# Raw weights in smaller paced transfers, 64-row products in chunk 0's joins, and sums of squares ahead of turned keys, in a fused DeltaNet and SiLU MLP kernel

## The chip, the cores and the metric

The kernel runs on one core of a Trainium2 chip. The metric is the device time of one execution in microseconds (us). Before the change the median of 3 runs is 650.97 us (650.86 to 651.51).

## What is computed

A DeltaNet recurrence over 768 tokens for 4 batches of 8 heads with 48 dimensions, and then a two-layer MLP with SiLU on all 3072 tokens (384 to 2048 to 384).

```python
k_n = k / (np.linalg.norm(k, axis=-1, keepdims=True) + 1e-06)
for t in range(S):
    kt, vt, bt = (k_n[:, :, t], v[:, :, t], beta[:, :, t, None])
    y[:, :, t] = np.einsum('bhd,bhde->bhe', q[:, :, t], state)
    v_old = np.einsum('bhde,bhd->bhe', state, kt)
    state = state + bt[:, :, :, None] * np.einsum('bhd,bhe->bhde', kt, vt - v_old)
x = y.transpose(0, 2, 1, 3).reshape(B * S, H * D)
h = x @ w_in
out = (h * (1.0 / (1.0 + np.exp(-h)))) @ w_out
```

## The kernel before

The tokens go in 6 chunks of 128, each in two halves of 64 (`hf`); the heads of all batches, 32 of them, go in two groups `g` of 16. Within a half the recurrence is solved in closed form: the products of the keys with each other (`score`, L519) form a triangular matrix per head, its inverse is built, and `inner`, `update`, `keys`, `old` and `new` then are matrix products with it. For chunk 0 the inverse starts from blocks of 16 by 16 on VectorE (`invert_first`, the pairs of operations at L666 and L670), which `joins` puts together to 32 by 32 and then to 64 by 64 on TensorE. Its stages follow one another for a half: `corner` of both groups (L707, evacuated at L714), `turned` of both (L723), `straight` (L736) and `merge_half` (L796), the last in two steps. Every stage's products go to PSUM; ScalarE (`by_act`) and VectorE (`by_dve`) copy the results out, and the next stage reads the copies. `corner`, `turned` and `straight` use 32-row operands: tiles `low`, `y` and `up` in a spare part of `sums_of_w`. One call of `corner` or `straight` has 32 products, of `turned` and `merge_half` 16.

`joins(0)` is run before any chunk's output; `joins(1)` is run in steps between other work. After `joins(0)` come `inner` (L830) and `first_outputs` (L874), and then the first products of the MLP (`hidden`, L1031).

Before the inversion, chunk 0's keys are squared on GpSimd (L375), summed on VectorE (`add_squares`, L379), and turned to norms (`norm_steps`, L393 to L413), of which `spread` goes through a product (`block_steps`, `pg`, L435) to the tile `step` that the inversion scales with. The keys are turned on TensorE (`turn`, L490) and copied out by VectorE (L502) or ScalarE (L504); `first_blocks` (L1274) multiplies them in blocks, and one transpose of VectorE (L1281) brings the blocks in. `busy` (L338) is a product that nobody reads; it fills TensorE's time.

The weights come as raw pairs of 32-bit words. `fetch_w_in` and `fetch_w_out` load piece `i` (768 KB) with one DMA into a buffer that happens to be free: a buffer of the hidden layer, half of a `w_out` buffer, or `sums_of_g`. `narrow` makes float32 of a piece in five steps: two on ScalarE (L226, L227), two on VectorE (L231, L235), one on GpSimd (L239). All loads are issued by SyncE in one line (`in_line`); `pace` makes the next one wait until the DMA before it has landed, and `linked` sets that for one transfer (L170 to L174).

The order of every engine's instructions is that of the program text: `pin` ties each to the one before it on its engine. In the middle of the program a long string of words, written by hand, gives that order (`script`): `s` a step of chunk 0's solution, `f` a step of narrowing, `r` a step of the MLP, `j` a product of `joins(1)`, `T` and `q` the turning of chunk 1's keys and queries, `l`, `p`, `i`, `m`, `t`, `z` steps of chunk 1's and 2's preparation and of the sums of weights. Chunks 1 to 5 follow in loops, with their own order.

Of the kernel before, what the change touches and what calls it, by code (L numbers as in the profile page):

```python
# [19 lines left out]
def kernel(  # L20
# [10 lines left out]
    nc = tc.nc  # L31
# [139 lines left out]
    def linked(fetch, *args):  # L171

        pace.append(line[-1])
        fetch(*args)  # L174

# [100 lines left out]
    def fetch_w_in(i):  # L276
# [8 lines left out]
        in_line(nc.sync.dma_start(out=raw, in_=src))  # L285
# [5 lines left out]
    def fetch_w_out(i):  # L291
# [5 lines left out]
        in_line(nc.sync.dma_start(out=raw, in_=src))  # L297
# [354 lines left out]

    def invert_first(step):
# [7 lines left out]
        for m in range(Q - 1, 0, -1):  # L661
# [39 lines left out]
        def corner(g, hf):  # L701

            pls = [bank(room, "pl") for room in (A, CC)]
            for i, n, k in heads(g, hf):
                for j in (2 * k, 2 * k + 1):
                    cols = slice(T * (j % 2), T * (j % 2 + 1))
                    pin(nc.tensor.matmul(  # L707
                        pls[k][rows[j], Q * i : Q * (i + 1)], lhsT=aps[0, g][0][rows[j], n % HH // H, n % H, cols],
                        rhs=low[rows[j], n, :], start=True, stop=True,
                    ))  # L710
                    yield
            for k in range(2):
                of = slice(W * k, W * (k + 1))
                pin(nc.vector.scalar_tensor_tensor(  # L714
                    out=of_half(y[of], g, hf, k)[:, :, 0:Q], in0=out_of(pls[k], of, Q), scalar=second[of],
                    in1=pick[of, 0:Q].unsqueeze(1).to_broadcast([W, HH // 2, Q]), op0=ALU.mult, op1=ALU.add,
                ))

        def turned(g, hf):

            pls = [bank(room, "pl") for room in (A, CC)]
            for i, n, k in heads(g, hf):
                pin(nc.tensor.matmul(  # L723
                    pls[k][rows[2 * k], T * i : T * (i + 1)], lhsT=up[rows[2 * k], n, :],
                    rhs=y[rows[2 * k], n, :], start=True, stop=True,
# [5 lines left out]
        def straight(g, hf):  # L731

            pls = [bank(room, "pl") for room in (A, CC)]
            for i, n, k in heads(g, hf):
                for j in (2 * k + 1, 2 * k):
                    pin(nc.tensor.matmul(  # L736
                        pls[k][rows[j], T * i : T * (i + 1)], lhsT=y[rows[j], n, :],
                        rhs=up[rows[j], n, :], start=True, stop=True,
                    ))
                    yield  # L740
# [568 lines left out]
    for t in xis:  # L1309
        pin(nc.gpsimd.memset(t, 0.0))  # L1310
    first_sizes = norm_steps(0)
# [4 lines left out]
    pools["m0"] = pools["m1"] = ctx.enter_context(tc.tile_pool(name="hiddens", bufs=1, space=PSUM))  # L1316
    fetch_w_in(0)
    load_k(1)
    fetch_w_in(1)
    load_v(0)  # L1320
    for c in range(1, NCH):
        beta_of(c)
    for b in range(2):
        first_score(b)
    busy(1)
# [261 lines left out]
```

## Time and profile before

| what | value |
|---|---|
| median of 3 runs | 650.97 us (650.86 to 651.51) |
| the profiled execution's own time | 653.34 us |
| its span | 651.4 us |
| granted TensorE clock, mean | 0.976 |
| PE busy (matmul) | 627.3 us, 96% |
| PEld busy (weight loads) | 550.7 us, 85% |
| DVE (VectorE) busy | 394.3 us, 61% |
| ACT (ScalarE) busy | 216.3 us, 33% |
| POOL (GpSimd) busy | 95.7 us, 15% |
| DMA | 53.68 MB, mean 82 GB/s |

Times in the profile are in us from the span's start unless they are marked ns. A row of the timeline has start, duration, engine, line, operation, result and operands, shape and count, and in brackets the idle time before it and what ended it. The releaser "issue" means that the engine waited for nothing that the profile shows. A window's row gives the busy time of each engine in a stretch. One product of 32-bit data appears as two matmuls and two weight loads; a transpose appears as one of each.

### The profile page before, as it was taken

The page shows a single profiled execution, that of the slowest core. Times are in us where ns is not written, and L with a number is a line of the kernel's source. Part 1 is how long each engine was busy: PE and PEld are TensorE (multiplying, and loading weights), DVE is VectorE, ACT ScalarE, POOL GpSimd, SP SyncE. Part 2 cuts the span into 40 slices and gives each one's busy share as a digit, 9 for nine tenths or more (in the row PEclk, how much of TensorE's full clock was granted, in tenths as well). Part 3 has the DMA queues.
Part 4 walks back from the last instruction along what each step waited for, and adds up shares of the span by engine and source line. Part 5 has one row for each costly group of instructions (what it writes and reads, how often), then busy time and mean ns, then how long its engine had stood idle before and what let it go on. Part 6 is the DMA issues. An engine that isn't in the chain of part 4 may idle for free.

```text
span 651.4 us, 21809 instructions
## 1 busy us (share of the span) xinstructions
PE 627.3 (96%) x9644; PEld 550.7 (85%) x9644; DVE 394.3 (61%) x902; ACT 216.3 (33%) x505; POOL 95.7 (15%) x96
## 2 busy tenths in 40 slices
PE   6859999999999999999999999999999999899997
PEld 4648778666789988989989989989989989789997
DVE  5955979988764985554975453986455963103112
ACT  1646666251351122451122451122451122351111
POOL 5231730337011020010020010020011000000000
PEclk9758999999999999999999999999999999999999
DMA  9675444160369433269243259334163023100101
GB/s 171 141 185 149 148 123 105 49 146 3 78 129 155 60 77 46 60 131 159 43 94 34 57 126 151 59 77 50 41 140 71 24 68 43 40 13 1 25 0 25
DMA packets 141310, 53.68 MB, mean 82 GB/s; under 512 B 112912, under 2 KB 134672, under 8 KB 141216
## 3 DMA queue, kind: packets, MB, share of 16 engines
q1 hardware_dynamic: 140880, 52.14, 40.1%
q8 instruction: 76, 1.25, 0.8%
q10 hardware_dynamic: 336, 0.15, 0.1%
q14 instruction: 18, 0.15, 0.1%
HBM read 39.62 MB, written 10.49 MB: 77 GB/s over the span
## 4 chain that ended last, share of the span: by engine, by line
PE 85%; DVE 8%; DMA 2%; issue 2%; ACT 1%; SPq 1%; POOL 0%; DVEq 0%; POOLq 0%
PE phid L1031 35%; PE px L1138 15%; PE py L1138 11%; PE po L1066 7%; PE pa L519 3%; PE pz L830 3%; DVE rank L617 2%; PE pu L850 2%; PE ph L818 2%; DVE x L622 2%; PE pyc L909 2%; PE pt L490 1%; PE pyc L896 1%; PE px L772 1%; PE py L772 1%
## 5 line engine op out<-in xcount | busy, mean ns | idle before, releaser
L1031 PE MATMUL phid<-xT,w_in 128*128 128x256 f32 x1152 | 258.4, 382 | 2.0 <-DMA xT<-part 2.0
L1031 PEld LDWEIGHTS phid<-xT,w_in 128*128 128x128 f32 x1152 | 215.9, 190 | 33.4 <-issue 3.5
L1041 ACT ACTIVATE gT<-phid 128x512 f32<-128x512 f32 x88 | 52.6, 598 | 143.6 <-PE phid L1031 140.8
L617 DVE SCALAR_TENSOR_TENSOR rank<-g,step,x 128x31 f32<-128x31 f32 (+15 forms) x124 | 49.8, 401 | 35.6 <-DMA g<-blocks 32.2
L1120 DVE TENSOR_TENSOR sums_of_g<-gT 128x384 f32<-128x384 f32 (+1 forms) x60 | 30.1, 521 | 58.9 <-ACT gT L1041 48.3
L1138 PE MATMUL px<-sums_of_w,sums_of_g 128*128 128x192 f32 x320 | 56.8, 329 | 0.0
L1138 PE MATMUL py<-w_out,sums_of_g 128*128 128x192 f32 x320 | 56.8, 329 | 0.0
L1138 PEld LDWEIGHTS px<-sums_of_w,sums_of_g 128*128 128x128 f32 x320 | 52.2, 190 | 0.5
L1138 PEld LDWEIGHTS py<-w_out,sums_of_g 128*128 128x128 f32 x320 | 52.2, 190 | 0.4
L622 DVE TENSOR_TENSOR x<-x,rank 128x31 f32<-128x31 f32 (+15 forms) x124 | 42.5, 342 | 4.3
L457 POOL TENSOR_TENSOR vf<-vf,n_slot 128x768 f32<-128x768 f32 x10 | 15.3, 1539 | 174.5 <-DMA vf<-in_v_dram 123.4
L478 DVE STREAM_TRANSPOSE kq<-stage 128x512 f32<-128x512 f32 x28 | 28.6, 1114 | 8.1 <-DMA stage<-in_q_dram 7.6
L534 ACT COPY xT<-pyc 48x128 f32<-48x128 f32 (+2 forms) x126 | 32.6, 259 | 1.6
L1138 PE MATMUL px<-sums_of_w,gT 128*128 128x192 f32 x160 | 28.4, 329 | 0.0
L1138 PE MATMUL py<-w_out,gT 128*128 128x192 f32 x160 | 28.4, 329 | 0.0
L1138 PE MATMUL px<-w_out,gT 128*128 128x192 f32 x160 | 28.0, 327 | 0.0
L830 PEld LDWEIGHTS pz<-vf,xi 64*64 64x64 f32 x768 | 25.2, 142 | 3.2 <-issue 2.9
L540 POOL COPY g<-x 64x256 f32<-64x256 f32 x4 | 5.0, 1240 | 151.9 <-DVE x L625 151.9
L1138 PEld LDWEIGHTS px<-w_out,gT 128*128 128x128 f32 x160 | 26.4, 190 | 0.5
L830 PE MATMUL pz<-vf,xi 64*64 64x48 f32 x768 | 26.9, 226 | 0.0
L1138 PEld LDWEIGHTS py<-w_out,gT 128*128 128x128 f32 x160 | 26.1, 190 | 0.3
L1138 PEld LDWEIGHTS px<-sums_of_w,gT 128*128 128x128 f32 x160 | 26.1, 190 | 0.2
(197 smaller groups left out, 833.8 us busy)
## 6 DMA issues: line engine op xcount, KB each, us to landing
vf<-in_v_dram SPq DMA_DIRECT2D x48, 96.0 KB, 3.3
out_dram<-o SPq DMA_DIRECT2D x42, 96.0 KB, 2.2
w_out<-in_moe_w_in_dram SPq DMA_DIRECT2D x4, 768.0 KB, 6.0
sums_of_w<-in_moe_w_out_dram SPq DMA_DIRECT2D x4, 768.0 KB, 4.9
blocks<-ap SPq DMA_DIRECT2D x40, 64.0 KB, 1.9
g<-blocks SPq DMA_DIRECT2D x5, 512.0 KB, 3.7
kb<-in_k_dram SPq DMA_DIRECT2D x12, 192.0 KB, 4.6
kb<-in_k_dram SPq DMA_DIRECT2D x24, 96.0 KB, 4.5
```

Of the source, the lines that this page charges most:

```text
L457: pin(nc.gpsimd.tensor_tensor(out=vf, in0=vf, in1=of, op=ALU.mult))
L478: pin(nc.vector.transpose(out=kqs[c, b][:, :, j, :].rearrange("p a (i m) -> p a m i", i=T), in_=src.rearrange("p a (m d) -> p a m d", d=D) ...
L519: pin(nc.tensor.matmul(pa[e][half, p * n * W : (p + 1) * n * W], lhsT=kq[rows, p, 0, half], rhs=kq[rows, p, js[0] : js[-1] + 1, half], sta ...
L534: return pin(nc.scalar.copy(to, of))
L617: pin(nc.vector.scalar_tensor_tensor(out=tv, in0=g[:, 0:m, m : m + 1].to_broadcast([P, m, n]), scalar=step[:, m : m + 1], in1=x[:, m : m + ...
L622: yield pin(nc.vector.tensor_tensor(out=x[:, 0:m, m:T], in0=x[:, 0:m, m:T], in1=tv, op=ALU.add))
L830: yield pin(nc.tensor.matmul(pz[rows, n * D : (n + 1) * D], lhsT=xis[g][rows, u * H + 2 * p + e, :], rhs=vfs[c][rows, hf, g * HB + u, p, : ...
L1031: pin(nc.tensor.matmul(ph[:, j * GT : (j + 1) * GT], lhsT=w_in[:, a, (2 * f + j) * P : (2 * f + j + 1) * P], rhs=xTs[c, hf][:, a, :], star ...
L1041: pin(nc.scalar.activation(out=hidden_of(c, hf, f), in_=ph[:], func=ACTF.Silu, scale=-0.5 if in_blocks(c) else 0.5))
L1066: pin(nc.tensor.matmul(pos[i][:, 0:DM], lhsT=hidden_of(0, hf, f // 2)[:, at : at + C], rhs=w_outs[f // HFF][:, f % HFF, :], start=(f == 0) ...
L1120: pin(nc.vector.tensor_tensor(out=sums_of_g[:, k, fs], in0=of[0], in1=of[1], op=op))
L1138: pin(nc.tensor.matmul(to, lhsT=at, rhs=quarter(f, *b) if isinstance(b, tuple) else sums_of_w[b][:, f], start=start and f == 0, stop=f == ...
```

## The change

- Each piece of `w_in` is loaded by three DMAs of 256 KB and each piece of `w_out` by two of 384 KB. A new list `depth` makes each DMA wait until the one two places before it in the line has landed; `deep` sets it for one fetch, and `fetch_w_out` always sets it. Chunk 1's keys now come ahead of piece 0 of `w_in`, v waits for piece 1 (`linked`), and pieces 5 and 6 change places.
- `corner` and `straight` take operands of 64 rows, one product in place of two. For this the left operands are block-diagonal: `wides` (four tiles: two halves of `wide`, `low_w` and `cross_w`) are filled with the identity `pick_w` on ScalarE ahead, `lows` holds zeros in the other block, and two memsets zero the other block of `ap` before the corners. An evacuation of `corner` is now four operations of 32 partitions instead of two of 64.
- VectorE's four sums of squares stand ahead of the later key copies, which all go to ScalarE; the first `beta_of` comes ahead of the last `first_blocks`; one `busy` product after these becomes three, and one more stands in the inversion.
- The scores of chunk 0 and the turns of its queries have another order among the inversion's steps, the calls between the joins too, and the hand-written order of the middle part is another.

```diff
-    line, pace = [], []
+    line, pace, depth = [], [], []
...
-        if pace:
-            behind(dma, pace.pop(), Sync)
+        if pace or depth:
+            behind(dma, pace.pop() if pace else line[-2], Sync)
...
+    def deep(fetch, *args):
+
+        depth.append(True)
+        fetch(*args)
+        depth.pop()
...
-        in_line(nc.sync.dma_start(out=raw, in_=src))
+        for a in range(NKT):
+            in_line(nc.sync.dma_start(out=raw[:, a], in_=src[:, a]))
...
-        in_line(nc.sync.dma_start(out=raw, in_=src))
+        depth.append(True)
+        for a in range(2):
+            in_line(nc.sync.dma_start(out=raw[:, a], in_=src[:, a]))
+        depth.pop()
...
+    pick_w = const.tile([P, W], FP32, name="pick_w")
+    pin(nc.gpsimd.memset(pick_w[:], 0.0))
+    for j in range(NB):
+        rows, cols = slice(T * j, T * (j + 1)), slice(T * (j % 2), T * (j % 2 + 1))
+        pin(nc.gpsimd.tensor_copy(out=pick_w[rows, cols], in_=ident[rows, rows]))
...
-        low = sum_room[:, AT_LOW : AT_LOW + BH * Q].rearrange("p (n s) -> p n s", s=Q)
-        y = sum_room[:, AT_G : AT_G + BH * T].rearrange("p (n s) -> p n s", s=T)
...
-        pin(nc.vector.transpose(out=low.rearrange("p n s -> p s n"), in_=x[:, 0:Q, :]))
-        pin(nc.gpsimd.tensor_copy(
-            out=y[:, :, Q:T], in_=pick[:, Q:T].unsqueeze(1).to_broadcast([P, BH, Q])
-        ))
+        lows = sum_room[:, AT_G : AT_G + BH * T].rearrange("p (n i s) -> p n i s", i=2, s=Q)
+        for j in (0, 2):
+            pin(nc.gpsimd.memset(lows[rows[j], :, 1], 0.0))
+        pin(nc.vector.transpose(out=lows[:, :, 0].rearrange("p n s -> p s n"), in_=x[:, 0:Q, :]))
+        for k, by in enumerate((by_act, by_dve)):
+            by(lows[rows[2 * k + 1], :, 1], lows[rows[2 * k + 1], :, 0])
...
-                for j in (2 * k, 2 * k + 1):
-                    cols = slice(T * (j % 2), T * (j % 2 + 1))
-                    pin(nc.tensor.matmul(
-                        pls[k][rows[j], Q * i : Q * (i + 1)], lhsT=aps[0, g][0][rows[j], n % HH // H, n % H, cols],
-                        rhs=low[rows[j], n, :], start=True, stop=True,
+                half = HALVES[k]
+                pin(nc.tensor.matmul(
+                    pls[k][half, T * i : T * (i + 1)], lhsT=aps[0, g][0][half, n % HH // H, n % H, :],
+                    rhs=lows[half, n].rearrange("p i s -> p (i s)"), start=True, stop=True,
+                ))
+                yield
+            for k in range(2):
+                for odd in range(2):
+                    of, at = rows[2 * k + odd], T * odd
+                    pin(nc.vector.scalar_tensor_tensor(
+                        out=wides[g, hf ^ k ^ g][of, :, at : at + Q],
+                        in0=out_of(pls[k], of, T)[:, :, Q * odd : Q * (odd + 1)], scalar=second[of],
+                        in1=pick[of, 0:Q].unsqueeze(1).to_broadcast([T, HH // 2, Q]), op0=ALU.mult, op1=ALU.add,
...
-                for j in (2 * k + 1, 2 * k):
-                    pin(nc.tensor.matmul(
-                        pls[k][rows[j], T * i : T * (i + 1)], lhsT=y[rows[j], n, :],
-                        rhs=up[rows[j], n, :], start=True, stop=True,
-                    ))
-                    yield
+                half = HALVES[k]
+                pin(nc.tensor.matmul(
+                    pls[k][half, T * i : T * (i + 1)], lhsT=wide_of(n)[half],
+                    rhs=up[half, n, :], start=True, stop=True,
+                ))
+                yield
...
+    for b in range(B):
+        add_squares(0, b)
     for b in range(2):
         first_blocks(b)
     for b in range(2, B):
-        turn(0, b, 0, (A, CC)[b % 2], b % 2 == 0)
-    for b in range(2, B):
-        first_blocks(b)
-    for b in range(B):
-        add_squares(0, b)
+        turn(0, b, 0, (A, CC)[b % 2], False)
+    first_blocks(2)
     beta_of(0)
-    busy(1)
+    first_blocks(3)
+    busy(3)
     for t in xis:
         pin(nc.gpsimd.memset(t, 0.0))
+    wide_x = work.tile([P, HH, W], FP32, name="wide", tag="x", bufs=1)[:]
+    low_w = sum_room[:, AT_LOW : AT_LOW + BH * T // 2].rearrange("p (n s) -> p n s", s=W)
+    cross_w = crossed[:].rearrange("p n s -> p (n s)").rearrange("p (n s) -> p n s", s=W)
+    for to in (wide_x, low_w, cross_w):
+        pin(nc.scalar.copy(out=to, in_=pick_w[:].unsqueeze(1).to_broadcast([P, to.shape[1], W])))
...
+    load_k(1)
     fetch_w_in(0)
-    load_k(1)
     fetch_w_in(1)
-    load_v(0)
+    linked(load_v, 0)
...
-    linked(fetch_w_in, 2)
-    linked(load_q, 1)
+    deep(fetch_w_in, 2)
+    deep(load_q, 1)
     fetch_w_in(4)
-    linked(fetch_w_in, 3)
-    linked(fetch_w_in, 6)
-    linked(fetch_w_in, 5)
+    deep(fetch_w_in, 3)
+    deep(fetch_w_in, 5)
+    deep(fetch_w_in, 6)
...
-        for word in ["s2 u0", "u1", "w0", "s3 u2", "w1", "u3", "", "w2 w3", "", "", "", "", "", "", "", "", "", "", "", "", "", ""][n].split():
+        for word in ["s2 u0 u1 w0", "", "", "u2 s3", "", "", "w1 u3", "w2", "", "w3", "", "", "", "", "b", "", "", "", "", "", "", ""][n].split():
...
-    together(joins(0, [none, none, sizes_0, sized, filled(2), none, none, begin_next, filled(1), none]))
+    together(joins(0, [none, sizes_0, none, sized, none, filled(2), begin_next, none, none, filled(1)]))
```

The string of the middle part is replaced as a whole; it starts `s2 f2 s T f T q s q T j5 j16 j8 f j5 f r` before and `s2 f T T s q f q T j5 f j16 j8 f r j5 f b` after.

More of the change, by code (lines that the diff above doesn't have):

```diff
@@ L651, in corners, with wide_of @@
         return two[:, :, 0 : Q * T].rearrange("p i (s t) -> p i s t", t=T)[:, :, :, 0:Q]
+    wides = {}
+    def wide_of(n):
+        return wides[n // HH, n % 2][:, n % HH // 2]
     def invert_first(step):
@@ L724, in turned @@
                     pls[k][rows[2 * k], T * i : T * (i + 1)], lhsT=up[rows[2 * k], n, :],
-                    rhs=y[rows[2 * k], n, :], start=True, stop=True,
+                    rhs=wide_of(n)[rows[2 * k], 0:T], start=True, stop=True,
                 ))
@@ L1324 @@
         first_score(b)
+    for j in (1, 3):
+        pin(nc.gpsimd.memset(aps[0, 0][0][T * j : T * (j + 1), :, :, 0:T], 0.0))
     busy(1)
-    linked(fetch_w_in, 2)
-    linked(load_q, 1)
+    deep(fetch_w_in, 2)
+    deep(load_q, 1)
     fetch_w_in(4)
-    linked(fetch_w_in, 3)
-    linked(fetch_w_in, 6)
-    linked(fetch_w_in, 5)
+    deep(fetch_w_in, 3)
+    deep(fetch_w_in, 5)
+    deep(fetch_w_in, 6)
     begin(("in", 0))
@@ L1343 @@
         done = next(inv)
-        for word in ["s2 u0", "u1", "w0", "s3 u2", "w1", "u3", "", "w2 w3", "", "", "", "", "", "", "", "", "", "", "", "", "", ""][n].split():
+        for word in ["s2 u0 u1 w0", "", "", "u2 s3", "", "", "w1 u3", "w2", "", "w3", "", "", "", "", "b", "", "", "", "", "", "", ""][n].split():
             at = int(word[1:] or 0)
-            if word[0] == "b":
+            if word[0] == "s" and at % HB == 1:
+                first_score(at)
+                for j in (1, 3):
+                    pin(nc.gpsimd.memset(aps[0, at // HB][0][T * j : T * (j + 1), :, :, 0:T], 0.0))
+            elif word[0] == "b":
                 busy(1, done, Sync)
```

10 lines of the change are left out of this document (2 added, 8 removed).

## The prediction

> **What bounds the kernel now.** I read the page first: PE is busy 627.3 of the 651.4 us span, so 24.1 us of it is PE idle, and the chain that ended last is 85% PE. Then the windows, ten microseconds each, tell where the idle time lies (columns: stretch, length, busy time of PE, its weight loads, DVE, ACT, POOL, then granted TensorE clock, DMA share, GB/s):
>
> ```profile
> 10.00:20.00 10.00, 6.48 (x182) 4.66 (x183) 8.73 (x27) 1.78 (x8) 3.35 (x5) 0.75 1.08 196
> 20.00:30.00 10.00, 9.68 (x250) 7.38 (x242) 8.97 (x31) 8.52 (x21) 1.94 (x2) 0.74 0.73 163
> 30.00:40.00 10.00, 5.29 (x294) 4.88 (x295) 7.01 (x17) 2.95 (x7) 6.90 (x6) 0.60 0.67 151
> 40.00:50.00 10.00, 6.16 (x200) 5.82 (x201) 3.91 (x8) 4.96 (x11) 1.82 (x1) 0.50 0.60 170
> 50.00:60.00 10.00, 10.00 (x275) 9.00 (x272) 5.08 (x9) 5.60 (x12) 1.85 (x1) 0.87 0.60 167
> ```
>
> From 50 us on PE hardly stops (6.3 us idle from 200 to 651); between 10 and 50 us it idles 12.4 us, and the clock is granted at half speed for much of it. So the end moves one for one with the moment at which chunk 0's joins are through and PE becomes dense: the first product of `inner` (L830) at 47.57. The list of PE's waits from 0 to 60 us, longest first, says what holds it back:
>
> ```profile
> PE pl L723 <- issue: 2.8, 1, 2.8
> PE pw L338 <- POOL ident masks.py:199: 2.4, 1, 2.4
> PE px L796 <- issue: 2.4, 1, 2.4
> PE blocks L1274 <- issue: 2.3, 1, 2.3
> PE pl L736 <- issue: 2.1, 1, 2.1
> PE pg L435 <- DVE spread L413: 0.9, 1, 0.9
> ```
>
> "issue" means that PE waited for nothing that the profile shows, in mid-group. The timeline (start, duration, engine, line, operation, count, idle before) places them:
>
> ```profile
> 14.24 0.69 PE L1274 MATMUL blocks<-kq 48*32 48x32 f32 x56 [2.30 <-issue]
> ...
> 36.89 0.74 PE L723 MATMUL pl<-sums_of_w 32*32 32x32 f32 x21 [2.84 <-issue]
> ...
> 41.44 0.92 PE L736 MATMUL pl<-sums_of_w 32*32 32x32 f32 x53 [2.08 <-issue]
> ...
> 46.69 0.95 PE L796 MATMUL px<-xi,xe_y 32*32 32x32 f32 x26 [2.38 <-issue]
> 47.57 3.54 PE L830 MATMUL pz<-vf,xi 64*64 64x48 f32 x62
> ```
>
> Counting PE's records from the start (loads and matmuls; a product is two of each, a transpose one of each), these four stops come after 449, 1473, 1729 and 1985 instructions: all at 193 plus a multiple of 256. The page gives the other half:
>
> ```profile
> q8 instruction: 76, 1.25, 0.8%
> ```
>
> 76 packets of 16.4 KB for 19,288 PE instructions, 254 to a packet. The trace's packet records put one packet just ahead of each stop's end: they finish at 12.35, 35.36, 40.23 and 45.31, and PE resumes 1.2 to 1.9 us later. The packet for a block starts only after PE has crossed the boundary one block earlier; crossing to use takes 5.2, 6.1, 4.6 and 5.3 us. So 256 PE instructions cannot pass in less than about 5 us while DMA is this busy, and the joins' products pass in 1.3 us per 256. The Trainium skill (Runtime: NRT & Kernel Launch, Instruction fetch mechanics) says the same blocks of 256 are fetched while the last runs, the cost "mostly hidden"; this trace agrees on the block and not on the hiding, 9.6 us in four stops. By the page alone these stops would be no fetches, and fewer products would bring only their own PE time.
>
> **The change, part by part.**
>
> *Fewer products.* `corner` and `straight` go from 32 to 16 products a call. In `joins(0)` that is 64 products, 256 instructions, one block; the built program reaches `inner` at instruction 1782 instead of 2026, and the boundary 1985 falls behind it. The boundary 1473 moves from `turned` to the first merges, 1729 from `straight` into the last merge.
>
> *Sums of squares first.* Now DVE copies keys 2 (10.37 to 11.06) before the four sums end:
>
> ```profile
> 10.98 1.92 DVE L379 TENSOR_REDUCE ss<-sq 128x8 f32<-128x384 f32 x4
> 12.93 0.51 DVE L393 TENSOR_SCALAR seed<-ss 128x32 uint32<-128x32 uint32 x1
> 15.04 1.65 PE L338 MATMUL pw<-state,ident 128*128 128x384 f32 x2
> 17.56 0.60 PE L435 MATMUL pg<-pick,spread 128*128 128x32 f32 x2 [0.87 <-DVE spread L413]
> ```
>
> POOL's last square ends at 10.55, so the last sum can end near 11.05 and the spread be ready at 15.6 instead of 17.4: a gain of 1.9 us. But the filler product ahead of `pg` (L338) becomes three. Behind the stop that ends at 14.24 the last first-blocks end at 14.95; six matmuls at 0.70 us (4.21 us for six at 2.39, the half-speed row) end at 19.15, and the inversion's first operation goes from 18.80 to about 19.9: +1.1. At full clock they would take half, `pg` come at 17.1, and the inversion at 17.7: -1.1. The trace grants half from 15.05, so I take **+1.1** and keep -1.1. New on ACT are a third key copy (0.6) and three fills (1024 and twice 512 columns, 2.3 by the 512-column copies' 0.6); ACT is busy 1.78 of 10 us there. New on POOL are some 1.1 us of picks before 6.34 (it idles 2.06 there) and six small memsets (about 0.5 each by the 128x512 row) in place of a copy of 0.63, in 14.65 us of idle time: hidden. Without cover each would cost its own time.
>
> *DVE after the inversion.* A copy of 32x512 comes between the two transposes (between the 0.42 of 32x256 and the 1.05 of the 512-column transpose; 0.7 taken), and eight L714 operations of 32 partitions take the place of four of 64, same columns, 0.31 to 0.36 each: +1.4. The corner products then start at 32.1 (30.47 now), the eighth L714 ends near 36.6.
>
> *The joins.* Boundary 1217 is crossed in the corners at 32.5, so the next block is usable at 36.5 to 38.6 (4.0 to 6.1 us later; the low end is from the block after 61.41, which landed in 2.35 us, plus the 1.2 to 1.9 to its use). The products need it at about 38: turned 35.3 to 37.2, straight 0 to 37.7, then the merge. The block after that, asked for at 38.2, is usable at 42.2 to 43.5 where the last merge wants it at 41: one stop of 1 to 2.5 us in place of three of 7.3. `inner` starts at 43.2 to 44.5; I take 43.8, **-3.8**. The order on ACT, a weight conversion of 1.9 us ahead of the second merge's copy, lies inside that stop.
>
> *Joins of the other half* run beside dense PE: 128 corner matmuls take 1.55 us and 128 straight ones 1.76; 64 matmuls of 64 rows take 1.08 by L818 each time: -1.1. DVE pays 1.4 more while busy 8 to 8.8 of 10 us; I charge 0.5: **-0.6**. Shallower queues should shorten a few later stops (0.9 at 92.6, 1.1 at 181.8; none to both): **-0.4**.
>
> *Transfers.* Weights went as 768 KB, one after another, 4.4 to 6.0 us each. Now three of 256 KB, two under way. Rows of one transfer: 48 KB 2.0 us, 256 KB 3.3, 512 KB 3.7 and 4.1, so some 1.9 us fixed and about 1 us per 256 KB, an estimate from these rows. Two under way give a transfer every 1.45 us, 4.3 us per 768 KB: no worse. With v linked behind weight piece 1 (landed 24.05) and issued at 0.65 us each, v lands near 32, piece 2 near 37, the paced q near 46, pieces 4, 3, 5, 6, 7 near 49, 53, 58, 62 and 67. ACT took pieces 3 to 7 at 59.6, 64.1, 68.2, 73.4 and 75.1; moved up by 3.8 these stay later than the landings. Cost **0**, up to 10 in the rival below.
>
> Sum: -3.8 - 0.6 - 0.4 = -4.8, against the profiled execution's 653.34 (span 651.4 and 1.9 around it). The median of the runs shown is 650.97, 2.4 under it; the difference carries over, so 646.2, rounded to **646.0**.
>
> By the Trainium skill (DMA: Bandwidth & Descriptors, Rules for kernel authors) bandwidth wants 1 MiB or more per DMA, and small transfers should be made one large one, which speaks against splitting; no row here shows two transfers of 256 KB under way alone.
>
> **Rivals.**
> 1. *Filler at full clock.* If fewer stops keep the clock up, the inversion starts at -1.1 instead of +1.1 and the rest follows: -7, **644**. For it: an idle gap of 2.3 us alone dropped the clock. Against: that gap stays. Chance 0.22.
> 2. *Pacing starves the weights* (slower). If a 256 KB transfer takes 4.5 us as the 96 KB k rows do among others, two under way move 512 KB in 4.5 us, a piece takes 6.7 instead of 4.7, and q takes 13.5 instead of 7.6. Piece 3, behind q and piece 4, then lands some 10 us late, ACT's queue waits for it, and 2.8 us are spare (53 against 59.6 - 3.8): +7.5 - 4.8 = +3, **654**. It begins at a landing of 3.1 us (1.5 landings are 4.7 us) and has eaten the gain at about 4.0. For it: k, q and v rows of 96 KB take 3.3 to 4.9 us here. Against: those have 192-byte packets and up to eight under way; 256 KB alone takes 3.3. Chance 0.14. The large-transfer rule above is this rival.
> 3. *Stops only move.* If every block keeps taking 6.1 us and the +1.1 and +2.1 on DVE are paid in full, `inner` starts at 32.5 + 12.2 + 1.3 = 46: -1.6 and DVE's full 1.4 takes the joins' gain: about -1, **650**. Chance 0.16.
>
> Forecast 0.48. The range, **641 to 652.5**, holds the forecast, rivals 1 and 3, and the near part of 2. Faster than 649.7 (0.2%, about what a measurement of this kernel can tell from no change): forecast, rival 1 and a third of rival 3, 0.75; within: 0.11; slower 0.14.
>
> **What would show it.** Right: two of the four issue stops gone from the PE waits before 60 us, the remaining ones again at 193 plus a multiple of 256; L830's first product near 44; seed near 11.1; `pg` near 19 with 0.5 granted. Wrong: ACT's conversions or SP waiting for weight transfers with PE idle after 50 us (rival 2), `pg` near 17 (rival 1), L830 near 46 (rival 3). What would overthrow the reading itself: stops at other counts, or the same stops with the end unmoved.

## The result and the profile after

The changed kernel takes 656.88 us (median of 6 runs, 654.13 to 659.46) against 651.32 for the kernel before (6 runs, 650.86 to 652.17): ratio 1.0088, 95% interval 1.0066 to 1.0111. It is slower by 5.6 us where 5.0 less were forecast. The profiled execution took 656.33 us, its span 654.6, 1.7 around it.

The page of the changed kernel first, its row of busy times and the row of instruction fetches:

```profile
PE 633.4 (97%) x9394; PEld 556.0 (85%) x9394; DVE 394.3 (60%) x910; ACT 219.1 (33%) x510; POOL 98.6 (15%) x106
...
q8 instruction: 74, 1.21, 0.8%
```

PE has 250 matmuls fewer and two blocks of instructions fewer than before (627.3 us, 76 packets), and yet it is busy 6.1 us longer. Its idle time falls from 24.1 to 21.2. Against this one execution of before the loss is in busy time; a second execution of before, shown below, was busy for 628.8 us and idle for only 20.4. The windows from 10 to 60 us, columns as before (length, then PE, its loads, DVE, ACT, POOL, clock, DMA share, GB/s):

```profile
10.00:20.00 10.00, 8.13 (x208) 5.59 (x208) 7.64 (x29) 4.83 (x16) 3.01 (x5) 0.83 1.11 180
20.00:30.00 10.00, 6.88 (x211) 5.25 (x210) 9.08 (x28) 8.07 (x20) 3.96 (x7) 1.00 0.50 138
30.00:40.00 10.00, 9.05 (x238) 8.59 (x240) 8.83 (x22) 3.75 (x8) 6.99 (x6) 0.66 0.58 145
40.00:50.00 10.00, 8.87 (x210) 8.56 (x206) 4.55 (x9) 5.04 (x11) 1.83 (x1) 0.50 0.51 133
50.00:60.00 10.00, 9.99 (x199) 8.24 (x197) 6.01 (x13) 6.18 (x11) 1.85 (x1) 0.98 0.58 182
```

From 30 to 50 us PE is now busy 17.9 of 20 us (11.5 before) with fewer matmuls (448 for 494), in part because more of `inner` now lies in this stretch, in part because the products of the joins take longer. PE's waits to 60 us, longest first:

```profile
PE pa L534 <- ACT kq L515: 2.4, 1, 2.4
PE pw L353 <- POOL ident masks.py:199: 2.4, 1, 2.4
PE blocks L1295 <- issue: 1.7, 1, 1.7
PE px L817 <- ACT xe_y L549: 1.1, 1, 1.1
PE pl L744 <- DVE sums_of_w L734: 0.9, 1, 0.9
PE pl L726 <- ACT sums_of_w L549: 0.6, 1, 0.6
```

Of the four "issue" stops one is left, after 449 instructions; the three in the joins are gone. The wait at the last merge (L817) is for ACT's copy. The timeline has the filler matmuls (now L353) and `pg` ahead of the inversion, then of the joins `corner` (L726) and half of `straight` (L757), and the first rows of `inner` (now L851):

```profile
13.72 3.43 PE L353 MATMUL pw<-state,ident 128*128 128x384 f32 x6
16.99 0.30 PE L450 MATMUL pg<-pick,spread 128*128 128x32 f32 x2
...
30.07 2.14 PE L726 MATMUL pl<-sums_of_w,ap 64*64 64x32 f32 x64 [0.64 <-ACT sums_of_w L549]
...
34.95 1.92 PE L757 MATMUL pl<-sums_of_w,wide 64*64 64x32 f32 x32
...
43.64 3.54 PE L851 MATMUL pz<-vf,xi 64*64 64x48 f32 x62
```

`inner` starts at 43.64, forecast 43.8. But 64 corner matmuls take 2.14 us where the 128 of before took 1.30, and 32 of `straight` take 1.92, 60 ns each at half clock. (A corner matmul also moves twice the columns now, 32 for 16; one of `straight` moves 32 in both kernels.)

Following three milestones shows where the gain goes: the first corner product, `inner`'s first, and `hidden`'s first for the second half (its 97th matmul). The table has the profiled execution of each kernel below, one for each. "Busy" is the time in which at least one matmul runs and "idle" the rest of the stretch, in us; a wait ahead of the first corner product is not in it.

| kernel | first corner | corner to inner: us, busy, idle | inner to hidden's second half: us, busy, idle |
|---|---|---|---|
| before | 30.47 | 17.10, 9.02, 8.08 | 52.58, 51.14, 1.44 |
| before, second execution (e5) | 30.43 | 13.61, 8.70, 4.91 | 52.52, 51.20, 1.32 |
| before, third (e10, alike up to here) | 30.45 | 15.28, 8.66, 6.62 | 52.50, 51.26, 1.24 |
| changed | 30.07 | 13.56, 11.56, 2.00 | 57.38, 54.49, 2.89 |
| changed again (e16) | 30.37 | 14.77, 12.41, 2.36 | 56.40, 53.50, 2.91 |
| e1, 32-row products | 30.45 | 13.03, 8.69, 4.34 | 56.94, 52.36, 4.58 |
| e2, 64-row products alone | 31.67 | 13.40, 11.70, 1.69 | 54.91, 53.28, 1.63 |
| e4, sums alone | 30.46 | 16.87, 9.29, 7.59 | 52.19, 50.91, 1.28 |
| e6, changed, old transfers | 29.32 | 14.37, 11.76, 2.61 | 57.27, 54.36, 2.91 |
| e8, changed, old order | 31.02 | 14.56, 13.12, 1.44 | 56.12, 53.64, 2.47 |
| e9, order alone | 30.49 | 15.21, 8.97, 6.24 | 61.21, 55.27, 5.94 |
| e11, sums and transfers | 30.01 | 13.42, 9.47, 3.95 | 56.69, 52.79, 3.91 |
| e14, changed, crosswise | 30.54 | 14.03, 10.01, 4.02 | 59.57, 54.82, 4.75 |
| e15, 64 rows alone, crosswise | 30.78 | 12.57, 10.55, 2.02 | 56.20, 52.11, 4.09 |
| e17, text of the middle alone | 30.20 | 17.10, 9.03, 8.07 | 58.88, 52.96, 5.92 |

Two things stand out. First, the joins of the same kernel before took 17.10, 13.61 and 15.28 us: they differ by 3.5 us between executions, 3.1 of it in the three stops, and the one that I worked from was the worst of the three. Second, the stretch behind `inner`, 52.5 us in all three executions of before, takes 56.4 to 57.4 in the changed kernel. Against the second execution of before, whose 650.98 us is the time of the median before the change (on the chip that it ran on the median was 652.55), the changed kernel is 0.4 ahead at the first corner, gains nothing in the joins (13.56 against 13.61), loses 4.9 up to hidden's second half, 0.6 from there to hidden's 217th matmul and 0.3 to the last chunk: 5.4 in all, close to the 5.6 between the medians. Of the 4.9, 1.6 is idle time and 3.3 is busy time: 1.4 in the joins' products (`pl`), 1.2 in the turns of chunk 1 (half clock lasts to 50.4, to 47.9 there), 0.8 in the scores (`pa`), 0.4 in the merges, less 0.5 in others. The 1.2 of the turns depends on the execution: in e16, the same kernel, it is 0.4.

Single executions carry this only so far. e11 has neither the 64-row products nor the new order, and it too takes 56.69 us behind `inner`, with a half-clock stretch (71.59 to 75.01) and three stops in them (PE's waits from 44 to 101 us):

```profile
PE pa L529 <- issue: 2.1, 1, 2.1
PE pl L717 <- issue: 0.8, 1, 0.8
PE pu L860 <- issue: 0.6, 1, 0.6
```

Steadier is the moment at which hidden's second half begins: 96.6 to 100.2 us in the five executions with 32 rows and the old order (the three of before, e4, e11), 101.0 to 101.5 in the two of the changed kernel and in e6.

### The profile page after: what moved, and what is told of

It reads as the page before. It is cut to its first block, busy times and chain, and to the rows that moved or that the text cites. A ratio compares the mean times of both kernels' runs of the same rounds, so it can differ in the third digit from the quotient of the medians.

```text
span 654.6 us, 21391 instructions
## 1 busy us (share of the span) xinstructions
PE 633.4 (97%) x9394; PEld 556.0 (85%) x9394; DVE 394.3 (60%) x910; ACT 219.1 (33%) x510; POOL 98.6 (15%) x106
## 4 chain that ended last, share of the span: by engine, by line
PE 70%; DVE 13%; SPq 5%; DMA 4%; ACT 3%; issue 2%; POOL 1%; DVEq 0%; POOLq 0%; ACTq 0%
PE phid L1052 25%; PE px L1159 12%; PE py L1159 9%; PE po L1087 6%; DVE rank L632 4%; DVE x L637 3%; PE pz L851 3%; PE pa L534 2%; SPq L910 2%; PE ph L839 2%; SPq L104 2%; PE pyc L930 2%; PE pu L871 1%; DVE sums_of_g L1141 1%; DMA up<-x 1%
## 5 line engine op out<-in xcount | busy, mean ns | idle before, releaser
L851 PEld LDWEIGHTS pz<-vf,xi 64*64 64x64 f32 x768 | 26.3, 148 | 3.4 <-issue 3.2
L851 PE MATMUL pz<-vf,xi 64*64 64x48 f32 x768 | 27.9, 232 | 0.0
```

Of the source, the lines that this page charges most:

```text
L851: yield pin(nc.tensor.matmul(pz[rows, n * D : (n + 1) * D], lhsT=xis[g][rows, u * H + 2 * p + e, :], rhs=vfs[c][rows, hf, g * HB + u, p, : ...
```

## The experiments

Fifteen kernels, all but e5 and e10 timed against the kernel before on the same chip (its median there 652.4 to 652.8, single executions 648.9 to 657.8). The ratios and intervals are those on record; a ratio is not the quotient of the two medians, which is 1.0060 for e6 and 1.0023 for e2 and within 0.1% of the ratio for the others. The part of the change that each has (e12 and e13 have none of it and follow below):

| kernel | 64 rows | sums first | transfers | order | us | ratio, 95% |
|---|---|---|---|---|---|---|
| changed | yes | yes | new | new | 656.88 | 1.0088 (1.0066 to 1.0111) |
| e16 changed again | yes | yes | new | new | 658.02 | 1.0076 (1.0052 to 1.0100) |
| e1 | no | yes | new | new | 655.80 | 1.0057 (1.0030 to 1.0083) |
| e2 | yes | no | old | old | 654.08 | 1.0039 (1.0004 to 1.0074) |
| e4 | no | yes | old | old | 654.03 | 1.0024 (0.9995 to 1.0053) |
| e6 | yes | yes | old | new | 656.45 | 1.0084 (1.0055 to 1.0113) |
| e8 | yes | yes | new | old | 656.61 | 1.0065 (1.0036 to 1.0094) |
| e9 | no | no | old | new | 659.85 | 1.0101 (1.0069 to 1.0134) |
| e11 | no | yes | new | old | 653.84 | 1.0018 (0.9989 to 1.0046) |
| e14 | four tiles | yes | new | new | 657.79 | 1.0079 (1.0048 to 1.0111) |
| e15 | four tiles | no | old | old | 654.13 | 1.0033 (1.0010 to 1.0056) |
| e17 | no | no | old | middle only | 659.39 | 1.0097 (1.0063 to 1.0131) |

The theories numbered in the expectations: 1, the 64-row products use two of PE's tiles in turn and cost more than the 32-row ones that they replace; 2, the transfers; 3, where the half-clock stretches fall; 4, the new hand-written order; 5, sums first. A product's tile on PE is the rows of its operands by the columns that its result takes: `corner` and `straight` use four tiles in turn with 32 rows and two with 64.

Where 32-row products meet the new text (e1, e9, e17), one step of `joins(1)` issues two of them; where 64-row products meet the old text (e2, e8, e15), one takes two steps. So each text reaches the stages at the words that it was written for.

### e1, 32-row products back

```diff
-                    pls[k][half, T * i : T * (i + 1)], lhsT=aps[0, g][0][half, n % HH // H, n % H, :],
-                    rhs=lows[half, n].rearrange("p i s -> p (i s)"), start=True, stop=True,
...
+                for j in (2 * k, 2 * k + 1):
+                    cols = slice(T * (j % 2), T * (j % 2 + 1))
...
+                    pls[k][rows[j], Q * i : Q * (i + 1)], lhsT=aps[0, g][0][rows[j], n % HH // H, n % H, cols],
+                    rhs=low[rows[j], n, :], start=True, stop=True,
```

> The changed kernel with the corner and straight products of chunk 0 back at 32 rows (two for each of 64 rows); sums first, transfers and the order of the middle stay. Theory 1 (the 64-row products use only two tiles of PE in turn, and each takes two to three times as long as a 32-row one on four): in the joins of the first half a product takes 10 to 15 ns again instead of 34 and 58, but the fetch stops come back there, so inner starts near 46 instead of 43.6; in the joins of the other half 1.6 us of PE time go, so hidden's first product of the second half is at 99 instead of 101. Time 650 to 652. Theory 2 (the transfers cost the time): 655 to 657 as the changed kernel. Theory 3 (where the half-clock stretches fall decides): the time follows the granted clock and not the joins; anything from 650 to 657, with stretches at half clock after 100 us wherever it is over 653.

Measured 655.80, ratio 1.0057: much of the loss stays without the 64-row products of `corner` and `straight`. `inner` starts at 43.49, earlier than expected, since the stops of this execution were short (1.2, 1.1 and 1.0 us). By the ratios (1.0088 and 1.0076 against 1.0057) theory 1 explains a quarter to a third of the loss, with an error as large. The stretch behind `inner` stays long (56.94), with PE waits of 1.5, 1.0, 0.8 and 0.7 us in it: PE is busy 2.1 us less than in the changed kernel and idle 1.7 more. So the exchange brings waits of its own, and the difference may understate what the 64-row products cost. No half-clock stretch begins there (that of the joins ends at 49.92), so theory 3 does not explain it either.

### e2, 64-row products alone

```diff
+    pick_w = const.tile([P, W], FP32, name="pick_w")
...
+                half = HALVES[k]
+                pin(nc.tensor.matmul(
+                    pls[k][half, T * i : T * (i + 1)], lhsT=aps[0, g][0][half, n % HH // H, n % H, :],
```

> The kernel before with the 64-row corner and straight products alone (fillers, wide tiles and small memsets that they need; before's sums, transfers and hand-written order). Theory 1: inner starts 2 to 3 us earlier than before's 47.57 (three stops gone, products slower), the joins of the other half give 2 to 5 us back; time 651 to 654, and a product of the corner takes 34 ns at full clock. My prediction's step (1.08 us for 64 such products at dense PE) would give 647 to 649. Theory 2 (transfers): 650 to 651.5, no loss. Theory 3: stretches at half clock after 100 us if it is over 653.

Measured 654.08, ratio 1.0039 (1.0004 to 1.0074): just over theory 1's range, and far from the 647 to 649 of the prediction's step. A part comes from the experiment itself: in before's order GpSimd's memset of `ap` comes late, and PE waits for it (the kernel's PE waits to 60 us):

```profile
PE pl L716 <- POOL ap L1359: 1.4, 1, 1.4
```

The first corner product is at 31.67 by that, 1.2 later than in before. So e2 and e8, which have this wait, overstate the products; changed against e1 (1.0088 and 1.0076 against 1.0057) does not have it, but has e1's own waits against it: 0.2 to 0.3%, with intervals of 0.25% on each.

### e6, old transfers

```diff
-        for a in range(NKT):
-            in_line(nc.sync.dma_start(out=raw[:, a], in_=src[:, a]))
+        in_line(nc.sync.dma_start(out=raw, in_=src))
```

> The changed kernel with raw weights in one transfer of 768 KB each, one after another, and the loads issued in the order of before; 64-row products, sums first and the hand-written order stay. Theory 1: as the changed kernel, 655 to 658. Theory 2: 650 to 652. Theory 3: the stretches at half clock after 100 us move or go with the traffic; without one, 653 to 655.

Measured 656.45, ratio 1.0084, against 1.0088 and 1.0076 of the changed kernel: theory 2, which wanted 650 to 652, falls. In the changed kernel 256 KB land in 3.1 us (median of the twelve that go to `w_out` buffers), the second rival's starting point, and PE never waits for a weight transfer.

### e5 and e10, the products by themselves

```diff
+        for name, tiles, wide in (
+            ("two_64", ((0, 0), (2, 2)), W), ("four_64", ((0, 0), (2, 2), (0, 2), (2, 0)), W),
+            ("two_32", ((0, 0), (2, 2)), T), ("four_32", ((0, 0), (2, 2), (1, 1), (3, 3)), T),
+            ("one_64", ((0, 0),), W), ("two_64_again", ((0, 0), (2, 2)), W),
+        ):
...
+                    banks_of[a // 2][to, at : at + T], lhsT=xis[0][of, n, 0:wide], rhs=xis[1][of, n, 0:T],
```

> The kernel before plus six sets of 128 products between dense work near the end, which nothing reads (output unchanged): 64 rows by 64 columns in turn on two tiles of PE (rows 0 and 64 to the same columns), on four (also crosswise), on one; 32 rows by 32 columns on two and on four diagonal tiles; each with 32 columns moving. Theory 1: two_64 30 to 36 ns a product, four_64 15 to 19, two_32 15 to 20, four_32 10 to 15, one_64 60 to 75, so the time of a set goes with the number of tiles in turn, 4.5 us for two_64 against 2.2 for four_64. If 64-row products are slow for themselves (rows, not tiles): four_64 as slow as two_64. If the stages of the joins, not the products, are slow: all sets 15 to 19 ns. The whole time grows by 15 to 25 us.

In e5 the sets stood behind a condition that never held, and none was issued: it is one more execution of the kernel before, 650.98 us. As such it is the most useful run of all. Its PE waits to 60 us:

```profile
PE blocks L1274 <- issue: 2.6, 1, 2.6
PE pw L338 <- POOL ident masks.py:199: 2.4, 1, 2.4
PE pl L736 <- issue: 1.5, 1, 1.5
PE pl L723 <- issue: 1.4, 1, 1.4
PE px L796 <- issue: 1.3, 1, 1.3
```

The same four stops at the same products, but the three in the joins are 4.2 us together instead of 7.3. `inner` starts at 44.03, 3.5 us earlier, and the execution ends 2.4 us earlier; the rest goes in a half-clock stretch near 565 us that the other does not have. The 2.4 us are as much as lies between the profiled execution of before (653.34) and its median (650.97).

> The probe of the products once more: six sets of 128 products between dense work of the chunk before the last, which nothing reads (output unchanged), as expected of the first probe, which issued none of them: theory 1 says two_64 30 to 36 ns a product, four_64 15 to 19, two_32 15 to 20, four_32 10 to 15, one_64 60 to 75; if rows and not tiles count, four_64 takes as long as two_64. The whole time grows by 15 to 25 us.

In e10 the sets were issued. Each set has 256 matmuls; the trace cuts the names to their first word, and the shape tells 64 from 32 rows. PE's timeline (start, duration, operation, shape, count, idle before):

```profile
541.65 12.76 PE L1473 MATMUL two<-xi 64*64 64x32 f32 x253 [0.17 <-DMA xi<-up]
...
554.25 6.49 PE L1473 MATMUL four<-xi 64*64 64x32 f32 x253
...
561.87 2.21 PE L1473 MATMUL two<-xi 32*32 32x32 f32 x128 [0.26 <-issue]
565.34 1.42 PE L1473 MATMUL two<-xi 32*32 32x32 f32 x79 [1.26 <-issue]
...
568.82 1.93 PE L1473 MATMUL four<-xi 32*32 32x32 f32 x128 [1.40 <-issue]
572.29 1.29 PE L1473 MATMUL four<-xi 32*32 32x32 f32 x80 [1.54 <-issue]
573.51 27.41 PE L1473 MATMUL one<-xi 64*64 64x32 f32 x255
...
600.75 13.92 PE L1473 MATMUL two_again<-xi 64*64 64x32 f32 x255
```

Half clock was granted from 542.82 to 559.89 us and from 566.71 to 621.32. At half clock a 64-row matmul takes 107 ns on one tile, 50 to 55 on two and 25 on four; a 32-row one takes 15 on four (and 17 at full clock on two). So the time goes with the number of tiles in turn, as theory 1 says. `corner` and `straight` used four 32-row tiles, and with 64 rows they use two: one matmul of 54 ns replaces two of 15. The Trainium skill (TensorEngine Tiling (Array Packing), Key Properties) says that different tiles load and multiply in parallel; the trace agrees, and gives the price of having only two in turn.

The idle time of these rows shows more. The 32-row rows begin at 561.87, 565.34, 568.82 and 572.29: 3.47 us apart, 256 instructions each, behind an "issue" stop, in a stretch in which DMA is busy 2%. Instruction packets end at 563.97, 567.49 and 571.02, 1.3 us ahead of the next start. That fits the fetch of the prediction with almost nothing in its way, and 3.47 us is the shortest distance between two stops seen here. The total grew by some 80 us and not by 15 to 25, for two reasons: a product is two matmuls, where the expectation took the time of one, and half clock was granted for most of the stretch. The windows of that stretch:

```profile
570.00:580.00 10.00, 8.46 (x196) 8.26 (x189) 0.00 (x0) 0.00 (x0) 0.00 (x0) 0.50 0.01 3
580.00:590.00 10.00, 10.00 (x97) 10.00 (x96) 0.00 (x0) 0.00 (x0) 0.00 (x0) 0.50 0.00 0
```

PE is busy for all of the second window, and half clock is granted.

### e8, e9 and e17, the order

```diff
-        "s2 f T T s q f q T j5 f j16 j8 f r j5 f b q T j4 j20 r j8 j4 j16 ...
+        "s f2 s T f T q s q T j5 j16 j8 f j5 f r q T j20 j5 b r j8 j4 j16 ...
```

(Only the start of the text is shown. e8 has it with the steps beside the inversion and between the joins; e9 is the reverse on the kernel before, e17 the reverse of this text alone.)

> The changed kernel in the order of before: the steps beside the inversion and between the joins, and the hand-written order of the middle, are before's; 64-row products, sums first and the new transfers stay. Theory 4 (the new order leaves PE waiting, 2.6 us idle between 70 and 100 us against 0.7, most of it for the mask of the next chunk's scores, and 0.8 more at 182 us): the stretch from inner's first product to hidden's first of the second half takes 54.5 to 55.5 us (57.4 in the changed kernel, 52.5 in the kernel before), and the time is 652.5 to 654.5, that of the 64-row products alone. Theory 1 alone (all the rest is the 64-row products): 656 to 658. Theory 5 (sums first costs): 655 to 657, with the inversion later than 17.6 or the first corner product later than 30.5.

> The kernel before with the new order alone (the steps beside the inversion, between the joins and in the middle); 32-row products, old sums, old transfers. Theory 4: 653.5 to 656, the stretch from inner to the second half 55.5 to 57 us. Theory 1 alone and theory 5: 650 to 652.5, the stretch 52.5 to 53.5.

> The kernel before with the hand-written text of the middle alone from the change (the steps beside the inversion and between the joins stay). If the text of the middle costs (theory 4): 655 to 660 as with the whole order (659.9), with the waits of PE at 65, 73 and 97 to 103 us that the whole order shows. If the steps beside the inversion and in the joins cost: 651 to 653.5.

e8 measured 656.61 (1.0065): above theory 4's range and in that of theory 1 alone and of theory 5. Its stretch behind `inner` is 56.12, 1.3 under the changed kernel's and not the 2 to 3 that theory 4 wanted, and PE waits 1.4 us for GpSimd's memset as in e2. e9 measured 659.85 and e17 659.39: on the kernel before, the text of the middle alone costs 1%, more than the whole change. PE's timeline of e17 has the largest single part of it:

```profile
65.80 0.37 PE L796 MATMUL py<-xe_y,ap 32*32 32x32 f32 x5 [2.09 <-issue]
...
67.00 2.43 PE L1031 MATMUL phid<-xT,w_in 128*128 128x256 f32 x6
```

The new text puts the products of `joins(1)` close together. With 32 rows they run into a fetch stop of 2.1 us (2.5 in e9), the clock falls to half from 65.54 to 68.95, and six matmuls of `hidden` take 2.43 us instead of 1.56. (Behind `inner` e17 is 6.3 us longer than before, 4.5 of it idle.) With 64 rows the same text has no stop there. So this 1% is not the order's share of the change. That share is e1 against e11 (+0.4%, with the stops that 32 rows meet in this text) and the changed kernel against e8 (+0.1 to 0.2%, too little by e8's memset). In the changed kernel the scores of chunk 1 wait longer, here with `pa`'s row of the groups from 44 us to hidden's second half, second execution of before (to 97 us) and changed kernel (to 101):

```profile
L519 PE MATMUL pa<-stage 48*64 48x64 f32 x256 | 5.6, 223 | 0.1
```

```profile
L534 PE MATMUL pa<-stage 48*64 48x64 f32 x256 | 6.2, 223 | 2.6 <-issue 1.1 <-ACT step L455 1.1 <-DVE vf L844 0.3
```

These are a stop after 4033 instructions (again 193 plus a multiple of 256) and a wait for ACT's copy of `step`, of the same size in e6 (1.15 and 1.08). The stop is not the order's alone: with the old order it is 0.1 to 0.9 us in the three executions of before, 1.4 in e8 and 2.1 in e11. The wait for `step`, 0.6 to 1.4 us, is found with the new text (changed, e1, e6, e9, e16, e17, though not in e14) and never with the old.

### e11 and e4, sums and transfers

```diff
+    for b in range(B):
+        add_squares(0, b)
     for b in range(2):
         first_blocks(b)
     for b in range(2, B):
-        turn(0, b, 0, (A, CC)[b % 2], b % 2 == 0)
+        turn(0, b, 0, (A, CC)[b % 2], False)
```

> The kernel before with sums first and the new transfers alone: 32-row products and before's order. It closes a square with the changed kernel (64 rows, new order: +0.9%), e8 (64 rows, old order: +0.65%) and e1 (32 rows, new order: +0.6%). If the 64-row products and the order carry the loss: 650 to 653, within 0.3% of before. If sums first or the transfers carry a part: 654 to 656.

> The kernel before with sums first alone. My prediction's +1.1 for it: 652 to 653.5, the inversion at 19.9. Rival 1 of the prediction (filler at full clock): pg near 17, the inversion near 17.6, 649.5 to 651.5. With e11 it gives the transfers' part by difference; theory: that part is within 1 us of none.

Measured 653.84 (1.0018) and 654.03 (1.0024), each within its error of none; the transfers' part by difference is -0.06%. e11 lies between its two ranges and e4 above both of its own; e4's inversion starts at 18.78, neither the 19.9 of the +1.1 nor rival 1's 17.6. The two do not carry the loss, though up to 0.5% lies inside their intervals.

### e12 and e13, chunk 1's keys turned earlier

```diff
+    together(joins(0, [
+        none, early(0), sizes_0, early(1, sized), filled(2), early(2), none, early(3, begin_next), filled(1), none,
+    ]))
```

(e12; in e13 the same four turns stand beside the inversion.)

> The kernel before with the four turns of chunk 1's keys (four transposes and a copy each) moved from the dense stretch behind inner to between the stages of the joins, before the fetch stops. If the stops are a floor on the time of 256 PE instructions (3.47 us in the probe without other DMA), the transposes cost nothing there and 1.8 to 2.3 us leave the dense stretch: the stops shrink by what the transposes take, 649 to 651 against 652.5. If the stops only move, or the copies of the turns delay the joins' own on ACT: 652 to 655.

> The kernel before with the same four turns beside the inversion, where PE waits for DVE: 1.8 to 2.3 us leave the dense stretch and nothing is added to the path, 649.5 to 651 against 652.5, if ACT's copies there do not hold the first corner products and the clock is not lower behind it. 652 to 654 if they do.

Measured 652.42 (0.9994, 0.9973 to 1.0014) and 653.56 (1.0009, 0.9987 to 1.0030): no gain. In e12 one stop of 2.6 us stays in the joins and the stretch behind `inner` is 52.77, as before: the transposes that left it were replaced by waits (idle 2.93 us instead of 1.44).

### e14 and e15, the 64-row products on four tiles

```diff
-                    pls[k][half, T * i : T * (i + 1)], lhsT=wide_of(n)[half],
+                    pls[k][HALVES[k ^ g], T * i : T * (i + 1)], lhsT=wide_of(n)[half],
...
+            both(corner), turned(0, hf), turned(1, hf), both(straight), merge_half(0, hf, False),
```

> The changed kernel with its 64-row products on four tiles: the corners of both groups are issued in turn, and the second group's products write the other half of their banks (read back from there), so rows 0 and 64 each go to both halves of the columns; straight likewise. Theory 1 (two tiles): a corner or straight product's matmul takes 15 to 18 ns at full clock and 25 to 30 at half instead of 34 and 58; some 2 us in the first half's joins (unless a fetch stop takes their place) and 2 us in the dense stretch go: 653 to 655 against 657 to 658 of the changed kernel again. If it is not the tiles: no change against the changed kernel, and the same ns for each.

> The kernel before with 64-row products on four tiles, nothing else of the change. Theory 1: 650.5 to 653, 2 to 3 us below the two-tile form of the same (654.1), and near or just under the kernel before, since a 64-row product on four tiles takes what two 32-row ones take. If it is not the tiles: 654 as the two-tile form.

> The changed kernel itself on this chip, beside the others: 656 to 659, 0.6 to 1.1% over the kernel before. If it is under 0.4%, the first result was of its chip.

Measured 657.79 and 654.13, against 658.02 (changed again) and 654.08 (e2): nothing gained, and theory 1's ranges for e14 and e15 were missed; e16 is inside its own. The products did get cheaper: `pl`'s busy time in the whole execution, without what overlaps, is 10.65 us in e14 against 13.67 in the changed kernel, and 10.94 in e15 against 14.31 in e2. But what they gave up came back as waits: PE idles for `pl` 5.04 instead of 1.51 us in e14, and 4.90 instead of 2.72 in e15. Two of e14's waits from 48 to 108 us:

```profile
PE px L817 <- DVE xe_y L552: 1.3, 1, 1.3
PE pl L744 <- DVE wide L734: 1.2, 1, 1.2
```

With both corners together DVE has eight evacuations of 32 partitions at a time, and `turned` waits for them. e14 also has half-clock stretches at 70.29 and 97.6. So the lower price of four tiles is shown, but this form also changes the order of the stages, and it does not show that the price of two tiles is what the change lost.

## Why the prediction was wrong

- **"The difference carries over"** is the first step that failed. The sum was -4.8 against an execution that was 2.4 us above its median, and it was carried to the median as it stood. But the 2.4 was mostly the stops: the second execution of before has 3.1 us less of them in the joins and ends 2.4 earlier. What the change could take from the stops was counted against an execution that had most of them. `inner` starts at 43.4 to 47.6 us in the eight executions with 32 rows there (e12 and e13 apart; mean 45.6) and at 43.6 to 45.6 in the five with 64 rows on two tiles (mean 44.6): the term of -3.8 is about -1.0.
- **Fewer products and the reading of the stops** held. The three stops in the joins went, the one left stands at 449, `inner` started at 43.64. The one stop forecast for the last merge did not come either; PE waits 1.1 us there for the copy on ACT that the prediction had placed inside that stop. The probe's stops, 256 instructions apart and 1.3 us behind a packet, bear out that they are fetches. The later stops were to get shorter (-0.4), and the one in the scores of chunk 1 did not: 1.1 us for 0.9.
- **"64 matmuls of 64 rows take 1.08 by L818 each time"** failed. L818 issues both groups in turn and uses four tiles; `corner` and `straight` use two. In the stretch behind `inner` 64 matmuls of `corner` advance PE by 2.21 us where 128 of 32 rows took 1.45, and `straight` by 2.33 against 1.48: +1.6 instead of -1.1. The nearest row was L830, two tiles, 57 ns at half clock, and it stood among the prediction's own lines. In the joins the same products took 5.84 us instead of 3.22, which used up most of the 2.9 us by which PE idled less there than in the second execution of before.
- **The hand-written order** was given no price, and it should have been a term: an order that places instructions for one count of fetch blocks meets other stops with another. It is some 0.1 to 0.4% here by the two pairs of kernels. That the other count of instructions is the reason is shown for e9 and e17; in the changed kernel the order's own wait, 1.1 us for `step`, is for ACT.
- **Sums of squares first** was priced at +1.1 because half clock was granted there in the trace of before. In the changed kernel `pg` came at 16.99 and the inversion at 17.55, rival 1's sign but not by its condition: half clock was granted from 12.82 to 16.23, the first four of the six filler matmuls ran in it, and only the last two, 0.33 us apart for 0.64, at full clock. They were early because the stop ahead of them ended at 12.95 and not at 14.24. In e16 all six ran at half clock and the inversion started at 18.30, in e4 at 18.78 (18.80 and 18.51 in two executions of before): the term is -1.2 to 0 and not +1.1. It brought 0.4 us at the first corner product (30.07) and in e4 nothing (30.46), where rival 1 gave 644 for the whole.
- **DVE after the inversion** held: from the inversion's first operation to the first corner product 12.2 us were forecast and 12.5 measured. The corner came at 30.07 and not at 32.1 because the inversion started earlier.
- **Transfers 0** held: v landed at 33.9, piece 7 at 67.1 (32 and 67 estimated), and e6 is no faster beyond its error. The rival that ended slower had the sign by luck, and not the mechanism. By the large-transfer rule of the Trainium skill (DMA: Bandwidth & Descriptors, Rules for kernel authors) e6 would have been faster; here splitting cost nothing that can be measured.

By the pairs, the 64 rows carry 0.2 to 0.3%, the order 0.1 to 0.4%, sums and transfers 0.2%, each about as large as its error, and they add to 0.5 to 0.9%. What stays open: the split is no sharper than that, the parts depend on each other, and why the crosswise form gives nothing back is argued from its waits alone.

## What to carry to other kernels

Before a stall is priced, compare the profiled execution's own time with the median: an execution that is late may be late in its stalls, as here, and they may not be there to be removed. Price a small product by a row with the same number of tiles in turn, not by one with the same rows. A hand-written order belongs to the instruction counts that it was made for, so carry it over or change it as a part with a price of its own.

## What the runs showed of the hardware

- In e10, with DMA busy 2%, PE resumes from four stops in a row 3.47 us apart, 256 instructions each; in the joins successive stops end 3.6 (e1) to 6.1 us (e10) apart. Between stops 256 instructions pass in 1.3 us (`corner` in the kernel before). The Trainium skill (Runtime: NRT & Kernel Launch, Instruction fetch mechanics) calls the cost of a boundary mostly hidden; for matmuls of 15 ns the measurement decides against it.
- The granted clock was 0.50 for 41 us in which PE was busy throughout, with 64-row matmuls on one and two tiles (e10, 573.5 to 614.6 us), and full clock came back 4.9 us after matmuls of 128 rows began (616.46, full at 621.32). There a busy PE was not enough for full clock.
- Executions of the kernel before differ by 3.1 us in the fetch stops of the joins (7.3, 5.9 and 4.2 us), and a half-clock stretch of 3.41 us near 565 us comes in one of them (e5, at 563.31) and not in the profiled one. It costs about 1.5 us: the part of the kernel in which it lies (from hidden's 961st to its 1001st matmul) takes 15.4 us in e5 and in the changed kernel, which has one at 569.19, and 14.0 and 13.9 in the profiled execution of before and in e16, which have none.
